# Block-sorted attention and a feed-forward on one core: sorting keys and values of batches 1 to 3 as rows, in tiles of the array, with crossbar transposes behind

## Chip, cores, metric

The kernel runs on 1 core of one Trainium2 chip. The metric is the device time of one execution in microseconds. Beside it stands the span of a profiled execution, from its first to its last instruction.

## What is computed

An attention over blocks with a learned soft sort, followed by a feed-forward over all tokens (3072 of them, 512 to 2048 features and back). There are 4 batches, 8 heads, 768 tokens and 64 features a head. Each head's tokens fall into 8 blocks of 96; an 8 x 8 matrix P (five rounds of normalising `sort_net` by rows and columns) mixes the blocks of keys and values, and then block i of the queries attends to mixed block i alone.

```python
def _attn_ref(q, k, v, sort_net):
    ...
    k_sorted = np.einsum('bhij,bhjcd->bhicd', P, k_b).reshape(B, H, S, D)
    v_sorted = np.einsum('bhij,bhjcd->bhicd', P, v_b).reshape(B, H, S, D)
    ...
    scores = scale * np.matmul(q_b, k_sb.transpose(0, 1, 2, 4, 3))
    scores = scores - np.max(scores, axis=-1, keepdims=True)
    attn = np.exp(scores)
    attn = attn / (np.sum(attn, axis=-1, keepdims=True) + 1e-09)
    return np.matmul(attn, v_sb).reshape(B, H, S, D).astype(np.float32)

def _moe_ref(x, w_in, w_out, s, b):
    h = x @ w_in
    r = np.maximum(h, 0.0)
    g = s * (r * r) + b
    return (g @ w_out).astype(np.float32)
```

## The kernel before

The feed-forward takes the tokens in eight tiles of 384, two a batch (`t = 2 * b` and `2 * b + 1`). `ffn1(t)` (line 395) makes 16 chunks of 128 hidden features, two per step, eight steps: 8 matmuls of 384 columns into a PSUM tile `hps`, a Relu on ScalarE (ACT) into `rt`, a squaring on VectorE (DVE) into `gt`. `ffn2(t)` (line 427) makes the output in three row groups of 128 tokens, each 16 matmuls of 512 columns into `ops`, followed by `store` (line 452): DVE scales `ops` into an `ot` tile (three buffers) and SP issues its DMA to `out`. Both take a table of slots: pieces of other work that are put into TensorE's stream after a step (`ffn1`) or after four matmuls (`ffn2`, slot = 4 * m + f // 4, so 12 slots in a call).

The attention of batch n = b + 1 is such other work: it lies in the slots of `ffn2(2 * b)` and `ffn2(2 * b + 1)`, and its result feeds `ffn1(2 * n)`. Each engine runs its instructions in the order in which they are written, with a wait at an instruction that needs another engine or a transfer. Batch 0's attention comes ahead of all that.

Attention of one batch:

- `load` (line 84) brings keys and values, cast to bf16, with partition = (head, block j, half z of the block) and 48 x 64 values in each; `load_q` (line 94) brings the queries in eight DMAs. GpSimd (POOL) issues these. For batches 2 and 3 they are behind `gated_loads` (line 555), whose small copy waits for the first `gt` of an earlier tile. Order in `loads` (line 508): k, v, q, then `v_sort`: eight copies on POOL that bring the values from (c, d) into (d, c) order, tile `VP`.
- `take_p` and `build_pd` (lines 219, 231) make `PD[b]`, a 128 x 128 matrix of weights from P, so that one matmul over the 128 partitions mixes the blocks of all heads. `jsel` and `bm` are masks for it; `emat` spreads P over the partitions.
- `k_piece` (line 247), three a batch: for each of 16 positions c, two matmuls with the raw keys as weights (128 x 64) and `PD` as the 64 moving columns. The result, keys with features on partitions, is in `tp`; the eviction reorders it into `KS`, where the 128 columns of one group g = (head pair, block) are contiguous (48 real and 16 zero columns, twice).
- `v_piece` (line 298), four a batch: for each of 16 features d, two matmuls with `VP` as weights and `PD` as 64 moving columns, into `tv`; the eviction reorders into `VS`, where a group's 64 features and two columns of ones lie side by side.
- `q_dma` (line 291): SP issues two DMA transposes of 96 x 2048 values through the crossbar, queries into `QT`.
- `s_piece` (line 311): 8 matmuls with weights from `KS` (64 rows x 128 columns) and 96 moving columns of `QT`; the two heads of a pair use the two halves of the rows. Then one Exp on ACT into `at`, 112 partitions.
- `p_piece` (line 342): 8 matmuls with `at` as weights and 66 moving columns of `VS`, then a reciprocal and a multiplication on DVE into `x`.
- `t_dma` (line 386): SP issues one DMA transpose of `x` into `xt`, which `ffn1` reads.

`KS`, `VP` and `VS` have two buffers each (`b % 2`). Tiles `tp`, `tv`, `sc`, `pv` and `hps` share three PSUM buffers of two banks (`psa`), taken in turn; `ops` has two of one bank (`psb`).

Of the kernel before, what the change touches and what calls it, by code (L numbers as in the profile page):

```python
# [22 lines left out]
def kernel(  # L23
# [33 lines left out]
    raw = [t.rearrange("b h (j z c) d -> b (h j z) (c d)", j=NB, z=2) for t in (q, k, v)]  # L57

    const = ctx.enter_context(tc.tile_pool(name="const", bufs=1))
    rawp = ctx.enter_context(tc.tile_pool(name="rawp", bufs=2))  # L60
# [23 lines left out]
    def load(t, b, parts=1):  # L84
# [3 lines left out]
        for c in range(0, C2, n):  # L88
            nc.gpsimd.dma_start(out=ti[:, c:c + n, :].rearrange("p c d -> p (c d)"),
                                in_=raw["qkv".index(t)][b][:, c * D:(c + n) * D])  # L90

    QTOK = {}

    def load_q(b, ns=range(NB)):
# [4 lines left out]
        for n in ns:  # L99
# [4 lines left out]
    nc.vector.memset(zeros[:, 128:512], 0.0)  # L104
    VP = [const.tile([128, D, GAP], BF, name=f"vp{i}") for i in range(2)]
    KS = [const.tile([128, NG, 2, GAP], BF, name=f"ks{i}") for i in range(2)]
    VS = [const.tile([KR, 2 * NG, VW], BF, name=f"vs{i}") for i in range(2)]
    nc.vector.memset(VP[0][:, :, C2:GAP], 0.0)
    nc.vector.memset(KS[0][:, :, :, C2:GAP], 0.0)
    nc.vector.memset(sne[:, NB, :], 1e-9)  # L110
# [6 lines left out]
    nc.gpsimd.memset(emat, 0.0)  # L117
    nc.gpsimd.affine_select(out=emat, in_=emat, pattern=[[-H, B], [-1, H], [0, 2 * NB]], base=0,
                            channel_multiplier=1, compare_op=ALU.not_equal, fill=1.0)
# [28 lines left out]

    def fill_vs(i):
        nc.gpsimd.memset(VS[i][:, :, D:VW], 1.0)  # L150
        nc.gpsimd.memset(VS[i][32:GAP, :, D:VW], 0.0)
        nc.gpsimd.memset(VS[i][32:C2, :, D:VW], 1.0)

    fill_vs(0)
    Z = []

# [7 lines left out]

    def permute(eng, b, src, cs=slice(0, C2), ds=slice(0, D)):
        o = VP[b % 2][:, ds, cs]
        i = src[:, cs, ds].rearrange("p c d -> p d c")
        if eng is nc.scalar:
            eng.copy(out=o, in_=i)
        else:  # L170
            eng.tensor_copy(out=o, in_=i)  # L171

# [3 lines left out]
    jsel = const.tile([128, NB], FP)  # L176
    bm = const.tile([128, 2 * 2 * NHP], FP)
    idle = [
        lambda: nc.vector.tensor_reduce(
# [9 lines left out]
    for it in range(5):  # L189
        nc.scalar.activation(out=sn, in_=sn, func=AF.Exp)  # L190
        if it >= 1:
            permute(nc.scalar, 0, v0f, slice((it - 1) * CV, it * CV))
# [25 lines left out]

    def take_p(b0, n, pe):

        bs = slice(b0, b0 + n)
        tmp = rtp.tile([128, n * NB, NB], FP, tag=f"tmp{n}", name="tmp")
        nc.vector.tensor_tensor(out=tmp, in0=pe.rearrange("p b i j -> p (b i) j"),
                                in1=spread(jsel, [[0, n * NB], list(jsel.ap[1])]), op=ALU.mult)
        nc.vector.tensor_reduce(out=PT[:, bs].rearrange("p b i -> p (b i)"), in_=tmp, axis=AX.X,
# [5 lines left out]
    def build_pd(b):  # L231
        pd = const.tile([128, 2, 2, NG], BF, name=f"pd{b}")
        nc.vector.scalar_tensor_tensor(
            out=pd.rearrange("p e z (a i) -> p (e z a) i", i=NB),
            in0=spread(bm, [list(bm.ap[1]), [0, NB]]), scalar=RC[:, b:b + 1],
            in1=spread(PT[:, b], [[0, 4 * NHP], list(PT.ap[2])]), op0=ALU.mult, op1=ALU.mult)
        PD[b] = pd

# [7 lines left out]

    def k_piece(b, c0, eng):
        src, mov, dst = RAW["k", b], PD[b], KS[b % 2]
        ps = psa.tile([128, CK, 2, NG], FP, tag="a", name="tp")
        for c in range(CK):  # L250
            for e in range(2):
# [3 lines left out]
                                 start=True, stop=True)  # L255
        evac(eng, dst[:, :, :, c0:c0 + CK], ps.rearrange("p c z g -> p g z c"))

    def q_tile(b):
# [38 lines left out]

    def v_piece(b, d0, eng):
        ps = psa.tile([128, CK, 2 * NG], FP, tag="a", name="tv")
        for d in range(CK):  # L300
            for z in range(2):
                nc.tensor.matmul(out=ps[z * GAP:(z + 1) * GAP, d, :],  # L302
                                 lhsT=VP[b % 2][:, d0 + d, :], rhs=PD[b][:, :, z, :],
                                 start=True, stop=True)
        evac(eng, VS[b % 2][:, :, d0:d0 + CK], ps[0:KR].rearrange("p d g -> p g d"))

# [4 lines left out]
    def s_piece(b, half, hp):  # L311
        g0 = hp * NB + half * HB
        sc = psa.tile([128, 2, 512], FP, tag="a", name="sc")
        for n in range(HB):
            for e in range(2):
                pr = slice(e * 64, (e + 1) * 64)
                nc.tensor.matmul(out=sc[:, e, n * BLK:(n + 1) * BLK],  # L317
                                 lhsT=KS[b % 2][pr, g0 + n].rearrange("p z c -> p (z c)"),
                                 rhs=QT[b][pr, half * HB + n, hp, :],
                                 start=True, stop=True)  # L320
        at = atp.tile([KR, 2, TG], BF, tag="at", name="at")
        nc.scalar.activation(out=at, in_=sc[0:KR, :, 0:TG], func=AF.Exp, scale=scale)  # L322
        AT[b, half, hp] = at

    def s_banks(b, half, hp):

        g0 = hp * NB + half * HB
        sc = [psb.tile([128, TG], FP, tag="b", name="scb") for _ in range(2)]
        for n in range(HB):
            for e in range(2):  # L330
                pr = slice(e * 64, (e + 1) * 64)
                nc.tensor.matmul(out=sc[e][:, n * BLK:(n + 1) * BLK],  # L332
                                 lhsT=KS[b % 2][pr, g0 + n].rearrange("p z c -> p (z c)"),
                                 rhs=QT[b][pr, half * HB + n, hp, :],
                                 start=True, stop=True)
        at = atp.tile([KR, 2, TG], BF, tag="at", name="at")
        for e in range(2):
            nc.scalar.activation(out=at[:, e], in_=sc[e][0:KR], func=AF.Exp, scale=scale)
        AT[b, half, hp] = at

    def p_piece(b, half, hp, later=False):
        g0 = hp * NB + half * HB
        atf = AT.pop((b, half, hp)).rearrange("p e t -> p (e t)")
# [4 lines left out]
        for e in range(2):  # L348
            for n in range(HB):
                c0 = (e * HB + n) * BLK  # L350
                m = 128 if c0 + 128 <= 2 * TG else BLK
                nc.tensor.matmul(out=pv[0:m, e, n * VW:(n + 1) * VW],  # L352
                                 lhsT=atf[:, c0:c0 + m], rhs=VS[b % 2][:, e * NG + g0 + n, :],
                                 start=True, stop=True)
# [103 lines left out]


    take_p(0, 1, spread_p(0, 1))  # L460
    build_pd(0)

# [4 lines left out]
    warm(3)  # L467
    k_piece(0, 0, "A")
    k_piece(0, CK, "D")
    k_piece(0, 2 * CK, "A")  # L470
    v_piece(0, 0, "D")
    v_piece(0, CK, "A")
    q_piece(0, 0, "D")
    v_piece(0, 2 * CK, "A")
    v_piece(0, 3 * CK, "D")
    s_piece(0, 0, 0)
# [31 lines left out]
    def loads(b):  # L508
        load("k", b)
        load("v", b)  # L510
        load_q(b)
        v_sort(b)

# [31 lines left out]
    def QB(b, n0, eng): return lambda: q_blocks(b, n0, eng)  # L545
# [16 lines left out]
    for b in range(B):  # L562
# [4 lines left out]
        if n == B:  # L567
# [44 lines left out]
```

## Time and profile before

| what | value |
|---|---|
| time, median of 3 runs | 228.32 us (227.29 to 228.38) |
| profiled execution: time, span | 228.41 us, 226.6 us |
| granted TensorE clock | 1.00 in every stretch |
| one batch in the steady part (start of `ffn2(0)` of one batch to the next) | 52.29, 102.30, 152.31: 50.01 us |
| of it `ffn1`, two tiles | 20.80 us |
| SP: DMA transposes of queries | 54.40 (two), 97.99 and 101.0, 148.0 and 150.7 |
| POOL: copies of `v_sort` | 52.90 to 59.34, 96.42 to 102.71, 146.29 to 152.57 |

The profile gives for each group of instructions its line, engine, operation, output and inputs, how many there were, the busy time, the mean of one in ns, and how long the engine sat idle before them and what ended that. Matmuls are pipelined, so the duration of a single one holds its way through the array; what a stream of them costs is read from the chain that ended last, which lists stretches by start and length. POOL's and SP's lines that end in `q` are the issuing of DMAs.

### The profile page before, as it was taken

The numbers are of one execution on the slowest core, as the hardware profiler recorded it, in microseconds if no ns is written. First come the engines' busy times: TensorE is split into PE (matmuls) and PEld (weight loads), VectorE is DVE, ScalarE is ACT, GpSimd is POOL, SyncE is SP. The second block draws the span as 40 slices with busy tenths as digits, with TensorE's granted clock in tenths as the row PEclk, the third lists the DMA queues.
The fourth block names the chain that finished last, engine by engine and source line by source line (L and its number), as shares of the span: only waits on it lengthen the run. The fifth ranks groups of instructions, "written<-read, shape, count | busy, mean of one in ns | idle before, by whom it ended". The sixth has DMA issues, their size and how long they took to land.

```text
span 226.6 us, 5806 instructions
## 1 busy us (share of the span) xinstructions
PE 218.9 (97%) x2542; PEld 133.2 (59%) x2542; DVE 124.5 (55%) x223; ACT 99.5 (44%) x128; POOL 68.2 (30%) x112
## 2 busy tenths in 40 slices
PE   7996999999999999999999999999999999999993
PEld 8985656655555556665555556655566566654452
DVE  6766467553647634498656634498557543441121
ACT  4966476564325225637143236627152246550000
POOL 8467797338400009291000028490000000000000
PEclk9999999999999999999999999999999999999999
DMA  5999999999711558993112459991123240001212
GB/s 190 238 105 133 181 164 206 207 196 136 164 49 49 129 151 136 188 166 72 49 47 73 138 120 176 176 171 36 49 95 67 100 114 0 4 0 46 94 49 93
DMA packets 53930, 25.82 MB, mean 114 GB/s; under 512 B 44944, under 2 KB 49296, under 8 KB 53904
## 3 DMA queue, kind: packets, MB, share of 16 engines
q0 software_dynamic: 30864, 12.85, 47.1%
q1 hardware_dynamic: 23040, 12.59, 20.9%
q8 instruction: 20, 0.33, 0.6%
q14 instruction: 6, 0.05, 0.1%
HBM read 27.27 MB, written 6.29 MB: 148 GB/s over the span
## 4 chain that ended last, share of the span: by engine, by line
PE 86%; DVE 5%; DMA 3%; POOL 2%; ACT 1%; issue 1%; POOLq 0%
PE ops L433 36%; PE hps L408 36%; PE pv L352 3%; PE tv L302 3%; DMA qtok<-in_q_dram 3%; PE sc L317 2%; PE tp L252 2%; PE ops L446 2%; POOL wi L131 1%; DMA sne<-in_sort_net_dram 1%; ACT rt L422 1%; POOL qtok L100 1%; ACT sne L190 1%; PE scb L332 1%; DVE rstat L200 0%
## 5 line engine op out<-in xcount | busy, mean ns | idle before, releaser
L408 PE MATMUL hps<-xt,wi 128*128 128x384 bf16 x512 | 85.7, 326 | 0.3 <-DMA qtok<-in_q_dram 0.3
L433 PE MATMUL ops<-wo,gt 128*128 128x512 bf16 x368 | 85.7, 379 | 0.0
L422 ACT ACTIVATE rt<-hps 128x768 bf16<-128x768 f32 x64 | 51.1, 811 | 53.4 <-PE hps L408 45.6
L423 DVE TENSOR_TENSOR gt<-rt 128x768 bf16<-128x768 bf16 x64 | 46.9, 739 | 41.2 <-ACT rt L422 40.4
L408 PEld LDWEIGHTS <-wi 128*128 128x128 bf16 x512 | 49.3, 98 | 33.5 <-issue 0.6
L433 PEld LDWEIGHTS <-gt 128*128 128x128 bf16 x368 | 33.7, 98 | 36.9 <-issue 0.6
L454 DVE SCALAR_TENSOR_TENSOR ot<-ops,s_bc,bias 128x512 f32<-128x512 f32 (+1 forms) x25 | 18.2, 730 | 30.8 <-PE ops L433 28.2
L322 ACT ACTIVATE at<-sc 112x768 bf16<-112x768 f32 x28 | 21.3, 808 | 30.3 <-PE sc L317 30.3
L100 POOL DMA_DIRECT2D qtok<-in_q_dram x32 | 24.9, 793 | 18.4 <-DMA rawv<-in_v_dram 9.0
L360 DVE TENSOR_TENSOR x<-pv,rec 96x512 bf16<-96x512 f32 x32 | 22.0, 687 | 1.1
L243 DVE CAST vs<-tv 112x1024 bf16<-112x1024 f32 x11 | 13.2, 1222 | 10.8 <-PE tv L302 10.7
L171 POOL COPY vp<-rawv 128x384 bf16<-128x384 bf16 x24 | 19.0, 849 | 0.0
L558 POOL COPY gate<-gt 128x1 bf16<-128x1 bf16 x2 | 0.4, 193 | 56.6 <-DVE gt L423 56.6
L352 PEld LDWEIGHTS <-at 112*128 112x128 bf16 (+1 forms) x256 | 12.8, 101 | 7.2 <-ACT at L322 1.1
L352 PE MATMUL pv<-vs,at 112*128 112x66 bf16 (+1 forms) x256 | 13.9, 195 | 1.0 <-DVE vs L243 1.0
L161 PE MATMUL z<-zeros 128*128 128x140 bf16 (+1 forms) x132 | 11.7, 256 | 1.2 <-DVE zeros L104 1.2
L302 PEld LDWEIGHTS <-vp 128*64 128x64 bf16 x512 | 9.0, 113 | 3.9 <-issue 3.6
L161 PEld LDWEIGHTS <-zeros 128*128 128x128 bf16 x132 | 10.1, 111 | 1.4 <-DVE zeros L103 1.0
L302 PE MATMUL tv<-pd,vp 128*64 128x64 bf16 x512 | 10.0, 197 | 0.9 <-issue 0.8
L241 ACT CAST ks<-tp 128x1024 bf16<-128x1024 f32 x8 | 8.1, 1012 | 4.0 <-PE tp L252 3.9
L131 POOL DMA_DIRECT2D wi<-in_moe_w_in_dram x16 | 8.6, 552 | 2.6 <-DMA wi<-in_moe_w_in_dram 0.9
L241 ACT CAST vs<-tv 112x1024 bf16<-112x1024 f32 x5 | 5.1, 1019 | 9.3 <-PE tv L302 9.3
(76 smaller groups left out, 104.3 us busy)
## 6 DMA issues: line engine op xcount, KB each, us to landing
out_dram<-ot SPq DMA_DIRECT2D x23, 256.0 KB, 2.0
qtok<-in_q_dram POOLq DMA_DIRECT2D x32, 96.0 KB, 9.5
rawk<-in_k_dram POOLq DMA_DIRECT2D x3, 768.0 KB, 6.8
rawv<-in_v_dram POOLq DMA_DIRECT2D x3, 768.0 KB, 10.0
wi<-in_moe_w_in_dram POOLq DMA_DIRECT2D x16, 128.0 KB, 5.2
wo<-in_moe_w_out_dram POOLq DMA_DIRECT2D x4, 512.0 KB, 10.8
v0f<-in_v_dram SPq DMA_DIRECT2D x4, 384.0 KB, 4.3
rawk<-in_k_dram POOLq DMA_DIRECT2D x3, 256.0 KB, 7.9
```

The source lines that it names most:

```text
L100: nc.gpsimd.dma_start(out=QTOK[b][:, n], in_=qv[:, n])
L161: nc.tensor.matmul(out=Z[0][:, 0:w], lhsT=zeros[:, 0:128], rhs=zeros[:, 0:w], start=True, stop=True)
L171: eng.tensor_copy(out=o, in_=i)
L302: nc.tensor.matmul(out=ps[z * GAP:(z + 1) * GAP, d, :], lhsT=VP[b % 2][:, d0 + d, :], rhs=PD[b][:, :, z, :], start=True, stop=True)
L322: nc.scalar.activation(out=at, in_=sc[0:KR, :, 0:TG], func=AF.Exp, scale=scale)
L352: nc.tensor.matmul(out=pv[0:m, e, n * VW:(n + 1) * VW], lhsT=atf[:, c0:c0 + m], rhs=VS[b % 2][:, e * NG + g0 + n, :], start=True, stop=True)
L360: nc.vector.tensor_tensor(out=x[:, :, hp * 128:(hp + 1) * 128].rearrange("p n (e d) -> p e n d", e=2), in0=pvv[:, :, :, 0:D], in1=rec.unsq ...
L408: nc.tensor.matmul(out=H1[i][:, f, 0:TG], lhsT=wi[:, hp, fc:fc + 128], rhs=xt[:, :, hp, :], start=(hp == 0), stop=(hp == NHP - 1))
L422: nc.scalar.activation(out=rt, in_=h, func=AF.Relu)
L423: nc.vector.tensor_tensor(out=gt[:, 2 * i:2 * i + 2, :], in0=rt, in1=rt, op=ALU.mult)
L433: nc.tensor.matmul(out=ops, lhsT=gt[:, f, m * 128:(m + 1) * 128], rhs=wo[:, f, :], start=(f == 0), stop=(f == NF - 1))
L454: nc.vector.scalar_tensor_tensor(out=ot[:, ns], in0=ops, scalar=s_bc, in1=BIAS[0][:, ns], op0=ALU.mult, op1=ALU.add)
```

## The change

Batch 0 stays as it is. In batches 1 to 3 keys and values are loaded with z as the slowest part of the partition, two DMAs of 64 partitions each (`load_z`), in the order k, q, v. `PD[b]` then is two 64 x 64 block matrices, one for each z, and it is the weights; the raw keys and values are the moving data. `k_rows` runs 16 matmuls a piece in tiles of 64 rows x 32 columns of the array, with 256 moving columns each; `v_rows` runs 4 in tiles of 64 x 64, with 384. The results have groups on the partitions, not features, so each piece is evicted into a staging place (`KO` and `VO`, batch 0's `KS` and `VP`), and SP issues DMA transposes of it into `KT` and `VT`: two for a piece of keys (128 x 512 each), one for a piece of values (128 x 1024). `keys` and `values` give the score and value matmuls their operands out of these: 128 columns of `KT` that lie 32 elements apart, and 66 columns of `VT` that lie 64 elements apart. The second buffers and `v_sort` go; the Exp of batches 1 to 3 is on 96 partitions. The masks for the new order are made by `masks_z` in `ffn1(1)`. The slots change: keys from slot 2 to 0, values from 5 and 9 to 6 and 8, the first `p_piece` from slot 11 of the first `ffn2` to slot 2 of the second, and `p_piece`s in pairs.

```diff
+    rawz = [t.rearrange("b h (j z c) d -> b z (h j) (c d)", j=NB, z=2) for t in (q, k, v)]
...
+    def load_z(t, b):
+        ti = rawp.tile([128, C2, D], BF, tag=f"raw{t}", name=f"raw{t}")
+        RAW[t, b] = ti
+        for z in range(2):
+            nc.gpsimd.dma_start(out=ti[z * 64:(z + 1) * 64].rearrange("p c d -> p (c d)"),
+                                in_=rawz["qkv".index(t)][b, z])
...
-    VP = [const.tile([128, D, GAP], BF, name=f"vp{i}") for i in range(2)]
-    KS = [const.tile([128, NG, 2, GAP], BF, name=f"ks{i}") for i in range(2)]
-    VS = [const.tile([KR, 2 * NG, VW], BF, name=f"vs{i}") for i in range(2)]
-    nc.vector.memset(VP[0][:, :, C2:GAP], 0.0)
-    nc.vector.memset(KS[0][:, :, :, C2:GAP], 0.0)
+    VP = const.tile([128, D, GAP], BF)
+    KS = const.tile([128, NG, 2, GAP], BF)
+    VS = const.tile([KR, 2 * NG, VW], BF)
+    nc.vector.memset(VP[:, :, C2:GAP], 0.0)
+    nc.vector.memset(KS[:, :, :, C2:GAP], 0.0)
+    KT = const.tile([128, 32, 128], BF)
+    VT = const.tile([128, D // 2 + 1, 128], BF)
+    KO = KS.rearrange("p g z c -> p (g z c)")[:, 0:C2 * D]
+    VO = VP.rearrange("p d c -> p (d c)").rearrange("p (d k) -> p d k", k=128)
...
-    nc.gpsimd.affine_select(out=emat, in_=emat, pattern=[[-H, B], [-1, H], [0, 2 * NB]], base=0,
+    nc.gpsimd.affine_select(out=emat[:, 0], in_=emat[:, 0], pattern=[[-1, H], [0, 2 * NB]], base=0,
...
+    for z in range(2):
+        em = emat[:, 1:B, z * 64:(z + 1) * 64]
+        nc.gpsimd.affine_select(out=em, in_=em, pattern=[[-H, B - 1], [-1, H], [0, NB]], base=-H,
+                                channel_multiplier=1, compare_op=ALU.not_equal, fill=1.0)
...
+    def masks_z():
+        nc.vector.tensor_reduce(
+            out=jselz, in_=ident.rearrange("p (z h j) -> p j z h", z=2, h=H), axis=AX.XY, op=ALU.add)
+        nc.vector.tensor_reduce(
+            out=bmz.rearrange("p (e a) -> p e a", e=2),
+            in_=ident.rearrange("p (z a e j) -> p e a z j", z=2, a=NHP, e=2), axis=AX.XY, op=ALU.add)
...
     def build_pd(b):
-        pd = const.tile([128, 2, 2, NG], BF, name=f"pd{b}")
+
+        m = bmz if b else bm
+        pd = const.tile([128, m.shape[1], NB], BF, name=f"pd{b}")
         nc.vector.scalar_tensor_tensor(
-            out=pd.rearrange("p e z (a i) -> p (e z a) i", i=NB),
-            in0=spread(bm, [list(bm.ap[1]), [0, NB]]), scalar=RC[:, b:b + 1],
-            in1=spread(PT[:, b], [[0, 4 * NHP], list(PT.ap[2])]), op0=ALU.mult, op1=ALU.mult)
-        PD[b] = pd
+            out=pd, in0=spread(m, [list(m.ap[1]), [0, NB]]), scalar=RC[:, b:b + 1],
+            in1=spread(PT[:, b], [[0, m.shape[1]], list(PT.ap[2])]), op0=ALU.mult, op1=ALU.mult)
+        PD[b] = (pd.rearrange("p (e a) i -> p e (a i)", e=2) if b else
+                 pd.rearrange("p (e z a) i -> p e z (a i)", e=2, z=2))
...
+    def k_rows(b, i, eng):
+
+        src = RAW["k", b]
+        ps = psa.tile([128, 2, CK // 4, 2, D], FP, tag="a", name="ko")
+        for e in range(2):
+            for x in range(4):
+                for z in range(2):
+                    zs, xs = slice(z * 64, (z + 1) * 64), slice(x * 32, (x + 1) * 32)
+                    nc.tensor.matmul(out=ps[xs, z, :, e, :], lhsT=PD[b][zs, e, :],
+                                     rhs=src[zs, i * CK + x:(i + 1) * CK:4, :],
+                                     start=True, stop=True, tile_position=(z * 64, x * 32))
+        ko = KO.rearrange("p (z m) -> p z m", z=2)[:, :, i * 512:(i + 1) * 512]
+        evac(eng, ko, ps.rearrange("p z c e d -> p z (c e d)"))
+        kt = KT[:, 0:C2 // 2].rearrange("p (z n) g -> p z n g", z=2)
+        for z in range(2):
+            nc.sync.dma_start_transpose(out=kt[:, z, i * 4:(i + 1) * 4, :], in_=ko[:, z])
+
+    def v_rows(b, i, eng):
+
+        src, n = RAW["v", b], D // 8
+        ps = psa.tile([128, 2, 512], FP, tag="a", name="vo")
+        for y in range(2):
+            for z in range(2):
+                zs, ys = slice(z * 64, (z + 1) * 64), slice(y * 64, (y + 1) * 64)
+                nc.tensor.matmul(out=ps[ys, z, 0:C2 * n], lhsT=PD[b][zs].rearrange("p e g -> p (e g)"),
+                                 rhs=src[zs, :, 2 * n * i + y:2 * n * (i + 1):2],
+                                 start=True, stop=True, tile_position=(z * 64, y * 64))
+        vo = VO[:, n * i:n * (i + 1), :]
+        evac(eng, vo[:, :, 0:BLK].rearrange("p d (z c) -> p z d c", z=2),
+             ps[:, :, 0:C2 * n].rearrange("p z (c d) -> p z d c", d=n))
+        nc.sync.dma_start_transpose(out=VT[:, n * i:n * (i + 1), :],
+                                    in_=vo.rearrange("p d k -> p (d k)"))
+
+    def keys(b, hp, n):
+
+        g = hp * NB + n
+        if b == 0:
+            return KS[:, g].rearrange("p z c -> p (z c)")
+        return KT.rearrange("p k (x g) -> p g (k x)", g=NG)[:, g]
+
+    def values(b, e, hp, n):
+        g = e * NG + hp * NB + n
+        if b == 0:
+            return VS[:, g, :]
+        return VT[0:BLK].rearrange("p d (y g) -> p g (d y)", y=2)[:, g]
+
+    def rows(b):
+        return BLK if b else KR
...
     def s_piece(b, half, hp):
-        g0 = hp * NB + half * HB
         sc = psa.tile([128, 2, 512], FP, tag="a", name="sc")
         for n in range(HB):
             for e in range(2):
                 pr = slice(e * 64, (e + 1) * 64)
                 nc.tensor.matmul(out=sc[:, e, n * BLK:(n + 1) * BLK],
-                                 lhsT=KS[b % 2][pr, g0 + n].rearrange("p z c -> p (z c)"),
+                                 lhsT=keys(b, hp, half * HB + n)[pr],
                                  rhs=QT[b][pr, half * HB + n, hp, :],
                                  start=True, stop=True)
-        at = atp.tile([KR, 2, TG], BF, tag="at", name="at")
-        nc.scalar.activation(out=at, in_=sc[0:KR, :, 0:TG], func=AF.Exp, scale=scale)
+        at = atp.tile([KR, 2, TG], BF, tag="at", name="at")[0:rows(b)]
+        nc.scalar.activation(out=at, in_=sc[0:rows(b), :, 0:TG], func=AF.Exp, scale=scale)
         AT[b, half, hp] = at
...
                 nc.tensor.matmul(out=pv[0:m, e, n * VW:(n + 1) * VW],
-                                 lhsT=atf[:, c0:c0 + m], rhs=VS[b % 2][:, e * NG + g0 + n, :],
+                                 lhsT=atf[:, c0:c0 + m], rhs=values(b, e, hp, half * HB + n),
                                  start=True, stop=True)
...
-    nc.gpsimd.memset(VP[1][:, :, C2:GAP], 0.0)
-    nc.gpsimd.memset(KS[1][:, :, :, C2:GAP], 0.0)
-    fill_vs(1)
+    nc.gpsimd.memset(KT[:, C2 // 2:, :], 0.0)
+    nc.gpsimd.memset(VT[:, D // 2, :], 1.0)
...
-    def v_sort(b):
-        for i in range(8):
-            permute(nc.gpsimd, b, RAW["v", b], ds=slice(i * 8, (i + 1) * 8))
-
     def loads(b):
-        load("k", b)
-        load("v", b)
+        load_z("k", b)
         load_q(b)
-        v_sort(b)
+        load_z("v", b)
...
-    def K(b, i, eng): return lambda: k_piece(b, i * CK, eng)
-    def V(b, i, eng): return lambda: v_piece(b, i * CK, eng)
...
-    ffn1(1, {-2: [TP(0, 1, 2, "D")], 1: [lambda: take_p(1, B - 1, PB), PDB(1)], 4: [PDB(2)],
+    ffn1(1, {-2: [TP(0, 1, 2, "D")], 1: [masks_z, lambda: take_p(1, B - 1, PB, jselz), PDB(1)], 4: [PDB(2)],
...
         q_dma(n)
         s0 = {
-            2: [K(n, 0, "A"), K(n, 1, "D"), K(n, 2, "A")],
-            5: [V(n, 0, "D"), V(n, 1, "A"), V(n, 2, "D")],
-            9: [V(n, 3, "D"), SC(n, 0, 0), SC(n, 0, 1)],
-            11: [P(n, 0, 0), SC(n, 0, 2), SC(n, 0, 3)]}
+            0: [K(n, 0, "A"), K(n, 1, "D"), K(n, 2, "A")],
+            6: [V(n, 0, "D"), V(n, 1, "A")],
+            8: [V(n, 2, "D"), V(n, 3, "A")],
+            10: [SC(n, 0, 0), SC(n, 0, 1)],
+            11: [SC(n, 0, 2), SC(n, 0, 3)]}
         ffn2(2 * b, s0)
-        ffn2(2 * b + 1, {0: [P(n, 0, 1)], 1: [P(n, 0, 2)],
-                         2: [P(n, 0, 3), TD(n, 0), SC(n, 1, 0), SC(n, 1, 1)],
-                         4: [P(n, 1, 0)], 5: [P(n, 1, 1), SC(n, 1, 2), SC(n, 1, 3)],
-                         7: [P(n, 1, 2)], 8: [P(n, 1, 3), TD(n, 1)]})
+        ffn2(2 * b + 1, {2: [P(n, 0, 0), P(n, 0, 1)],
+                         4: [P(n, 0, 2), P(n, 0, 3), TD(n, 0)],
+                         5: [SC(n, 1, 0), SC(n, 1, 1)], 6: [SC(n, 1, 2), SC(n, 1, 3)],
+                         8: [P(n, 1, 0), P(n, 1, 1)],
+                         10: [P(n, 1, 2), P(n, 1, 3), TD(n, 1)]})
```

More of the change, by code (lines that the diff above doesn't have):

```diff
@@ L147, in load_w @@
             nc.gpsimd.dma_start(out=wo[:, fs, :], in_=wov[:, fs, :])
[L149 to L154, printed above, removed]
+    nc.gpsimd.memset(VS[:, :, D:VW], 1.0)
+    nc.gpsimd.memset(VS[32:GAP, :, D:VW], 0.0)
+    nc.gpsimd.memset(VS[32:C2, :, D:VW], 1.0)
+    for z in range(2):
+        em = emat[:, 1:B, z * 64:(z + 1) * 64]
+        nc.gpsimd.affine_select(out=em, in_=em, pattern=[[-H, B - 1], [-1, H], [0, NB]], base=-H,
+                                channel_multiplier=1, compare_op=ALU.not_equal, fill=1.0)
     Z = []
@@ L162, in warm, with permute @@
                              start=True, stop=True)
[L165 to L171, printed above, removed]
+    def permute(cs):
+        nc.scalar.copy(out=VP[:, :, cs], in_=v0f[:, cs, :].rearrange("p c d -> p d c"))
     rstat = const.tile([BH, NB], FP)
@@ L177 @@
     bm = const.tile([128, 2 * 2 * NHP], FP)
+    jselz = const.tile([128, NB], FP)
+    bmz = const.tile([128, 2 * NHP], FP)
     idle = [
@@ L191 @@
         if it >= 1:
-            permute(nc.scalar, 0, v0f, slice((it - 1) * CV, it * CV))
+            permute(slice((it - 1) * CV, it * CV))
         if it in (1, 2):
@@ L217, in spread_p, with take_p @@
         return pe
-    def take_p(b0, n, pe):
+    def masks_z():
[4 more added lines that the diff above has]
+            in_=ident.rearrange("p (z a e j) -> p e a z j", z=2, a=NHP, e=2), axis=AX.XY, op=ALU.add)
+    def take_p(b0, n, pe, sel):
         bs = slice(b0, b0 + n)
@@ L223, in take_p @@
         nc.vector.tensor_tensor(out=tmp, in0=pe.rearrange("p b i j -> p (b i) j"),
-                                in1=spread(jsel, [[0, n * NB], list(jsel.ap[1])]), op=ALU.mult)
+                                in1=spread(sel, [[0, n * NB], list(sel.ap[1])]), op=ALU.mult)
         nc.vector.tensor_reduce(out=PT[:, bs].rearrange("p b i -> p (b i)"), in_=tmp, axis=AX.X,
@@ L245, with k_piece @@
     QT = {}
-    def k_piece(b, c0, eng):
-        src, mov, dst = RAW["k", b], PD[b], KS[b % 2]
+    def k_piece(c0, eng):
+        src, mov, dst = RAW["k", 0], PD[0], KS
         ps = psa.tile([128, CK, 2, NG], FP, tag="a", name="tp")
@@ L296, in q_dma, with v_piece @@
                 in_=QTOK[b][:, n0:n0 + HB].rearrange("p n h d -> p (n h d)"))
-    def v_piece(b, d0, eng):
+    def v_piece(d0, eng):
         ps = psa.tile([128, CK, 2 * NG], FP, tag="a", name="tv")
@@ L302, in v_piece @@
                 nc.tensor.matmul(out=ps[z * GAP:(z + 1) * GAP, d, :],
-                                 lhsT=VP[b % 2][:, d0 + d, :], rhs=PD[b][:, :, z, :],
+                                 lhsT=VP[:, d0 + d, :], rhs=PD[0][:, :, z, :],
                                  start=True, stop=True)
-        evac(eng, VS[b % 2][:, :, d0:d0 + CK], ps[0:KR].rearrange("p d g -> p g d"))
+        evac(eng, VS[:, :, d0:d0 + CK], ps[0:KR].rearrange("p d g -> p g d"))
     AT = {}
@@ L317, in s_piece @@
                 nc.tensor.matmul(out=sc[:, e, n * BLK:(n + 1) * BLK],
-                                 lhsT=KS[b % 2][pr, g0 + n].rearrange("p z c -> p (z c)"),
+                                 lhsT=keys(b, hp, half * HB + n)[pr],
                                  rhs=QT[b][pr, half * HB + n, hp, :],
                                  start=True, stop=True)
-        at = atp.tile([KR, 2, TG], BF, tag="at", name="at")
-        nc.scalar.activation(out=at, in_=sc[0:KR, :, 0:TG], func=AF.Exp, scale=scale)
+        at = atp.tile([KR, 2, TG], BF, tag="at", name="at")[0:rows(b)]
+        nc.scalar.activation(out=at, in_=sc[0:rows(b), :, 0:TG], func=AF.Exp, scale=scale)
         AT[b, half, hp] = at
     def s_banks(b, half, hp):
-        g0 = hp * NB + half * HB
         sc = [psb.tile([128, TG], FP, tag="b", name="scb") for _ in range(2)]
@@ L332, in s_banks @@
                 nc.tensor.matmul(out=sc[e][:, n * BLK:(n + 1) * BLK],
-                                 lhsT=KS[b % 2][pr, g0 + n].rearrange("p z c -> p (z c)"),
+                                 lhsT=keys(b, hp, half * HB + n)[pr],
                                  rhs=QT[b][pr, half * HB + n, hp, :],
                                  start=True, stop=True)
-        at = atp.tile([KR, 2, TG], BF, tag="at", name="at")
+        at = atp.tile([KR, 2, TG], BF, tag="at", name="at")[0:rows(b)]
         for e in range(2):
-            nc.scalar.activation(out=at[:, e], in_=sc[e][0:KR], func=AF.Exp, scale=scale)
+            nc.scalar.activation(out=at[:, e], in_=sc[e][0:rows(b)], func=AF.Exp, scale=scale)
         AT[b, half, hp] = at
     def p_piece(b, half, hp, later=False):
-        g0 = hp * NB + half * HB
         atf = AT.pop((b, half, hp)).rearrange("p e t -> p (e t)")
@@ L457, in store @@
         nc.sync.dma_start(out=out[r0:r0 + 128, ns], in_=ot[:, ns])
-    take_p(0, 1, spread_p(0, 1))
+    take_p(0, 1, spread_p(0, 1), jsel)
     build_pd(0)
@@ L467 @@
     warm(3)
[L468 to L472, printed above, removed]
+    k_piece(0, "A")
+    k_piece(CK, "D")
+    k_piece(2 * CK, "A")
+    v_piece(0, "D")
+    v_piece(CK, "A")
     q_piece(0, 0, "D")
-    v_piece(0, 2 * CK, "A")
-    v_piece(0, 3 * CK, "D")
+    v_piece(2 * CK, "A")
+    v_piece(3 * CK, "D")
     s_piece(0, 0, 0)
@@ L535, in make_bias, with K, V @@
         nc.scalar.activation(out=bias, in_=bps, func=AF.Copy, scale=b_bc)
-    def K(b, i, eng): return lambda: k_piece(b, i * CK, eng)
-    def V(b, i, eng): return lambda: v_piece(b, i * CK, eng)
+    def K(b, i, eng): return lambda: k_rows(b, i, eng)
+    def V(b, i, eng): return lambda: v_rows(b, i, eng)
     def SC(b, h, i): return lambda: s_piece(b, h, i)
```

## Prediction

> **What bounds the kernel now.** I read the busy times first, then the chain that ended last, then that chain by time through one steady batch, then single rows for the prices. Columns of the chain: start, length, engine, tile, line, count.
>
> ```profile
> PE 218.9 (97%) x2542; PEld 133.2 (59%) x2542; DVE 124.5 (55%) x223; ACT 99.5 (44%) x128; POOL 68.2 (30%) x112
> ...
> PE 86%; DVE 5%; DMA 3%; POOL 2%; ACT 1%; issue 1%; POOLq 0%
> ```
>
> TensorE is busy 97% of the span and makes 86% of the chain, so work taken from or given to TensorE in the steady part moves the end one for one, and work on other engines only where TensorE comes to wait for it. One batch of the steady part, 102.30 to 152.31 (three groups of the chain, from three places):
>
> ```profile
> 47.75 0.98 PE cps L527 x16
> ...
> 102.30 2.59 PE ops L433 x12
> 104.89 1.64 PE tp L252 x96
> 106.53 2.70 PE ops L433 x12
> 109.23 1.64 PE tv L302 x96
> 110.86 3.56 PE ops L433 x16
> 114.42 0.63 PE tv L302 x32
> 115.05 0.45 PE sc L317 x16
> ...
> 119.01 0.27 PE pv L352 x8
> ...
> 131.51 20.80 PE hps L408 x128
> ```
>
> There is no gap between the pieces: each starts where the last one ended. The sort of keys and values is 1.64 + 1.64 + 0.63 = 3.91 us of TensorE in each of batches 1 to 3. A lone matmul's price comes from two groups: ops takes 2.59/12 = 215.8 ns at 512 columns, hps 20.80/128 = 162.5 ns at 384, so 0.417 ns a column and 2.5 ns beside it. Against this, cps (four column tiles of the array, 512 columns) takes 0.98/16 = 61 ns a matmul, 3.5 at once. sc (two row tiles, 96 columns, 42.5 ns alone) takes 28 ns, two at once with 8 x 42.5 = 0.34 us and 0.11 us for going in and out of the tiled form. tp (two column tiles, 64 columns, 29.2 ns alone) takes 17 ns, also two at once.
>
> **The new sort on TensorE.** Keys: 3 pieces of 16 matmuls over 256 columns (109 ns alone), in 2 row x 4 column tiles. Eight at once gives 2 rounds a piece: 6 x 0.109 = 0.65, plus 0.11 for the form = 0.76. Two at once, the pairs of sc and tp, would be 24 x 0.109 + 0.11 = 2.73. Values: 4 pieces of 4 matmuls over 384 columns (162.5 ns), in 2 x 2 tiles: four at once 4 x 0.1625 + 2 x 0.11 = 0.87; two at once 1.52; one at a time 2.82. Row tiles overlap in sc and column tiles in cps, so I take full overlap: 0.76 + 0.87 = 1.63, which saves 3.91 - 1.63 = **2.28 us a batch**. Pairs alone would lose 0.34 a batch (2.73 + 1.52 - 3.91).
>
> **What reads the sorted data.** This is the hidden part. Today the evictions write the sorted rows so that each TensorE operand is contiguous. Now keys() takes 128 weight columns 64 bytes apart in KT, and values() takes 66 moving columns 128 bytes apart in VT. No TensorE row of this trace has such a stride. The nearest rows are other engines':
>
> ```profile
> L322 ACT ACTIVATE at<-sc 112x768 bf16<-112x768 f32 x28 | 21.3, 808 | 30.3 <-PE sc L317 30.3
> ...
> L169 ACT CAST vp<-v0f 128x768 bf16<-128x768 f32 x4 | 6.0, 1510 | 0.0
> ...
> L241 ACT CAST ks<-tp 128x1024 bf16<-128x1024 f32 x8 | 8.1, 1012 | 4.0 <-PE tp L252 3.9
> ```
>
> The cast of v0f reads elements 256 bytes apart. From 808 ns at 768 and 1012 at 1024, ScalarE pays 0.80 ns an element and 196 ns beside; the strided read pays (1510 - 196)/768 = 1.71 ns, 2.1 times as much. So three prices for a pv matmul, 64 of them a batch, 66 columns, 30.0 ns now: unchanged (+0); half rate, 0.833 ns a column, 57.5 ns (+27.5 x 64 = 1.76 us a batch); or ScalarE's time for an element on TensorE too, 1.71 ns, 115.4 ns (+5.46). I take half rate, the ratio of the nearest row, and keep both ends. The strided weights: two loads go under the 42.5 ns of a pair in sc. Unchanged they cost nothing; if each load came to 42.5 ns and the two went one after the other, a pair would take 85, +42.5 x 32 pairs = 1.36 us a batch. In pv a 128-column load hides under 31 ns, so there is room; I take nothing and keep 1.36. The moving rows of the new value sort have pairs 4 bytes apart; doubled they would be 0.65 more a batch, and I take nothing, as a line of neighbours is still used there.
>
> The Trainium skill's page SBUF — State Buffer (Door 1: The DMA port swizzle) speaks against the change: lines of 16 bytes, a stride free up to 8 bf16, a penalty for each access in a new line. It names no price for TensorE; by it, unchanged reads are out and the sum lies at the second or third price. On the weights, TensorE: Matmul & The Clock Gate (Weight-path perf modes) lets the fast load of 128 columns read packed or strided columns; by it their cost stays nothing.
>
> **The crossbar and its queue.** Each transpose of today moves 96 x 2048 values:
>
> ```profile
> L294 SPq DMA_TRANSPOSE qt<-qtok x6: 1424/1443/1686, 54.4 to 150.7; - x6
> ...
> DMA to landing us min/median/max: 3.7/3.8/4.2
> ```
>
> SP is held 1.44 us and the data lands 2.36 us later. New in a batch: six of 128 x 512 (a third of the data) and four of 128 x 1024 (two thirds). By size they hold SP 0.48 and 0.96 us each; by count 1.44. I take size, since both old shapes are equal and cannot separate the two. Count from T, the start of ffn2(2b), with 0.863 us per slot of four ops. Key evictions (1.01 ACT, 1.22 DVE) end at T+2.1, 2.6, 3.1; the six issues end at T+5.0 and land at T+7.4. Scores start after 11 slots and both sorts, 9.49 + 1.63 = T+11.1: 3.7 spare. Values are sorted at T+6.8 and T+9.0; their issues, with one output store (0.33) between, end at T+12.2 and land at T+14.5; the first pv comes after 15 slots, 1.63 and 0.90 of sc, T+15.5: 1.0 spare. By count, keys land at T+13.1 (2.0 late), values at T+19.6 (4.1 late in all): 4.1 us a batch. Behind a late transpose on SP wait the output stores, whose three ot buffers give slack of two row groups.
>
> **Loads, POOL, DVE, ACT.** POOL loses eight copies of 0.85 us a batch and gains two load issues of 0.56. Those copies lock the DVE today:
>
> ```profile
> 96.68 6.44 DVE L423 TENSOR_TENSOR gt<-rt 128x768 bf16<-128x768 bf16 x1 [0.74 <-ACT rt L422]
> ```
>
> One squaring that elsewhere takes 0.56 us takes 6.44 while POOL copies (96.42 to 102.71), and the last Relu of that stage runs at 105 instead of 103. TensorE never waits for it, so its end saves nothing by itself, but it lets the key sort move from slot 2 to slot 0: the PSUM buffers that it needs come free with Relus that now end by about T+1. If that cover failed, TensorE would wait some 2 us a batch. Queries now load ahead of the values; the last load lands where the last query load lands today (101.0 in batch 2, T-1.3; 54.4 in batch 1, T+2.1), while the value sort needs it at T+6.8, so 4.7 us cover it. Key loads stay first. In batch 1, the query transposes (54.4) stand ahead of the key transposes on SP: two issues, to T+5.0, so keys land by T+10.2, still 0.9 ahead. masks_z is two reductions near 0.27 us on a DVE busy 6.2 of 10 us there: nothing, 0.54 without that cover. Value evictions shrink from 1024 to 768 columns, off the chain. The split emat runs on POOL, which waits 4.78 us before line 463: nothing. Fewer, paired pv groups: 0.03 us each, left out.
>
> **Sum.** -2.28 + 1.76 = -0.52 a batch, three batches: -1.6 us. Profiled span 226.6 -> 225.0; that run took 228.41, 1.8 around the span, and the median of three is 228.32, so against the median **226.8 us**. By its unknowns: 226.8 + 3 x 1.36 = 230.9 with slow weight loads; 226.8 + 3 x 0.65 = 228.8 with slow moving pairs.
>
> **Rivals.** (1) Strides cost TensorE nothing: 228.3 - 6.8 = **221.5**. For it: pv and sc have the load hidden today and the operand rates of TensorE are its own; against: the strided ScalarE row. (2) Slower: a strided moving column costs what it costs ScalarE, 1.71 ns. -2.28 + 5.46 = +3.18 a batch, **237.9**. It decides from the point where a column of pv costs more than 0.96 ns (2.28 us over 64 x 66 columns is 0.54, plus today's 0.417). For it: the same row read as a time, not a ratio; against: TensorE already takes columns at half ScalarE's price. (3) Transposes cost SP their count, not their size: 226.8 + 12.3 = **239.1**, seen as TensorE waiting for KT and VT. Against: their data is a third. (4) Tiles overlap only in pairs: 228.3 + 3 x (0.34 + 1.76) = 234.6; cps speaks against it.
>
> **Chances.** Forecast 0.37, rival 1 0.28, rival 2 0.22, rival 3 0.09, rival 4 0.04. 0.5% (1.1 us) is what a measurement here tells from no change (the three runs lie 0.5% apart). The forecast lies just past it: of its 0.37, 0.20 falls faster, 0.12 within, 0.05 slower. Faster 0.28 + 0.20 = 0.48, same 0.12, slower 0.40. The range reaches rival 1 with a little room and rival 2: 220.5 to 238.5; the forecast's own is 225.5 to 230.9.
>
> **What would show it.** Chain of the new profile: key sort near 0.25 us a piece; an 8-group of pv at 0.27 (rival 1), near 0.5 (forecast) or 0.9 (rival 2); a 16-group of sc still 0.45 or toward 0.8 (weights); KT or VT as releaser of TensorE, and transposes of 1.4 us on SP, for rival 3; no gt of 6 us. I am wrong if the stride price is neither, or if something new holds TensorE in a batch.

## The result, and the profile after

The changed kernel takes 257.45 us (median of 6 runs, 255.62 to 258.99) against 228.35 us before: ratio 1.128, interval 1.1216 to 1.1343. The prediction was 226.8 us with a range of 220.5 to 238.5; the time lies outside it, and a gain was forecast where a loss came. The profiled execution's span is 253.9 us, 27.3 more than before.

The chain that ended last, by engine, on the page of the changed kernel:

```profile
PE 78%; DMA 6%; SPq 5%; DVE 4%; ACT 3%; issue 3%
```

TensorE's share fell from 86% to 78%; transfers and SP's issuing hold 11%, where transfers alone had 3%. The chain in order of time through batch 3 of the changed kernel (start, length, engine, tile, line, count; "issue" is time in which an engine waited for nothing that the profile shows):

```profile
171.74 0.81 PE ops L503 x3
172.55 0.78 PE ko L290 x48
...
178.67 1.26 SPq L297
179.93 0.05 issue
180.02 1.22 SPq L297
181.24 0.05 issue
181.29 2.48 DMA KT<-KS
183.77 0.35 issue
184.12 0.47 PE sc L389 x8
...
186.66 3.37 DMA VT<-VP
190.03 1.23 issue
191.25 1.98 PE pv L422 x16
193.23 2.92 PE ops L503 x8
...
199.62 0.81 PE ops L503 x3
200.43 0.63 PE sc L389 x14
...
202.89 1.82 PE pv L422 x16
```

Four things are to be seen. The key sort takes 0.78 us, where tp took 1.64. A pv matmul takes 1.82/16 = 114 ns, where it took 0.27/8 = 34. A 16-group of sc takes 0.63, where it took 0.45. And the chain leaves TensorE twice, for KT and for VT; after the second wait eight ops take 2.92 us instead of 1.73. The stretches of the changed kernel around that wait show why (columns: busy time of PE, PEld, DVE, ACT, POOL, then granted clock, DMA share, GB/s):

```profile
182.00:192.00 10.00, 6.91 (x59) 3.74 (x60) 0.96 (x2) 3.22 (x5) 0.00 (x0) 1.00 0.85 197
192.00:196.00 4.00, 4.00 (x20) 2.12 (x19) 2.52 (x5) 0.00 (x0) 0.00 (x0) 0.57 0.00 0
```

TensorE was busy for 6.91 of 10 us, and then the granted clock is 0.57 for a while: the wait is paid a second time. The transposes, as the changed kernel's tile view has them:

```profile
L297 SPq DMA_TRANSPOSE KT<-KS x18: 1190/1258/2018, 59.0 to 181.3; - x18
...
L312 SPq DMA_TRANSPOSE VT<-VP x12: 1272/1286/2147, 67.5 to 188.0; - x12
...
L367 SPq DMA_TRANSPOSE qt<-qtok x6: 3061/3896/4768, 50.9 to 170.1; - x6
```

SP is held 1.26 us by a transpose of 128 x 512 and 1.29 by one of 128 x 1024 (medians): between these two, size hardly matters.

### The profile page after: what moved, and what is told of

It is laid out like the page before. It is cut to its first block, busy times and chain, and to the rows that moved or that the text cites. A ratio compares the mean times of both kernels' runs of the same rounds, so it can differ in the third digit from the quotient of the medians.

```text
span 253.9 us, 4881 instructions
## 1 busy us (share of the span) xinstructions
PE 232.9 (92%) x2040; PEld 141.4 (56%) x2062; DVE 109.1 (43%) x222; ACT 101.1 (40%) x131; POOL 51.3 (20%) x93
## 4 chain that ended last, share of the span: by engine, by line
PE 78%; DMA 6%; SPq 5%; DVE 4%; ACT 3%; issue 3%
PE hps L478 32%; PE ops L503 27%; PE pv L422 10%; SPq L297 3%; PE sc L389 3%; DMA VT<-VP 3%; DMA KT<-KS 2%; DMA v0f<-in_v_dram 1%; PE ops L516 1%; SPq L312 1%; PE tv L375 1%; PE ko L290 1%; ACT at L394 1%; PE vo L306 1%; ACT rt L492 1%
## 5 line engine op out<-in xcount | busy, mean ns | idle before, releaser
L493 DVE TENSOR_TENSOR gt<-rt 128x768 bf16<-128x768 bf16 x64 | 35.5, 557 | 47.9 <-ACT rt L492 47.7
L394 ACT ACTIVATE at<-sc 96x768 bf16<-96x768 f32 (+1 forms) x28 | 21.2, 803 | 46.7 <-PE sc L389 46.5
L422 PEld LDWEIGHTS <-at 96*128 96x128 bf16 (+3 forms) x256 | 24.6, 112 | 10.7 <-issue 7.6
L422 PE MATMUL pv<-VT,at 96*128 96x66 bf16 x192 | 23.8, 290 | 6.0 <-DMA VT<-VP 3.2
L429 DVE RECIPROCAL rec<-pv 96x8 f32<-96x8 f32 x32 | 6.5, 202 | 30.3 <-PE pv L422 30.3
L389 PE MATMUL sc<-qt,KT 64*128 64x96 bf16 x192 | 8.8, 236 | 6.2 <-DMA KT<-KS 6.2
L389 PEld LDWEIGHTS <-KT 64*128 64x128 bf16 x192 | 7.2, 156 | 11.8 <-issue 11.4
L265 ACT CAST VP<-vo 128x768 bf16<-128x768 f32 x6 | 4.8, 799 | 17.3 <-PE vo L306 17.3
L267 DVE CAST VP<-vo 128x768 bf16<-128x768 f32 x6 | 5.7, 958 | 7.8 <-PE vo L306 7.8
L265 ACT CAST KS<-ko 128x1024 bf16<-128x1024 f32 x6 | 5.8, 1015 | 1.4 <-PE ko L290 1.4
```

The costliest lines, as they stand in the source:

```text
L265: nc.scalar.copy(out=out, in_=in_)
L389: nc.tensor.matmul(out=sc[:, e, n * BLK:(n + 1) * BLK], lhsT=keys(b, hp, half * HB + n)[pr], rhs=QT[b][pr, half * HB + n, hp, :], start=Tr ...
L394: nc.scalar.activation(out=at, in_=sc[0:rows(b), :, 0:TG], func=AF.Exp, scale=scale)
L422: nc.tensor.matmul(out=pv[0:m, e, n * VW:(n + 1) * VW], lhsT=atf[:, c0:c0 + m], rhs=values(b, e, hp, half * HB + n), start=True, stop=True)
L493: nc.vector.tensor_tensor(out=gt[:, 2 * i:2 * i + 2, :], in0=rt, in1=rt, op=ALU.mult)
```

## The experiments

The length of a batch goes from one start of ops after hps to the next, in each profile's chain; the table has batch 2, which the loading of weights no longer disturbs. Each ratio is to the old kernel as measured beside that run (228.35 to 229.51 us).

| kernel | time, us | ratio to before (interval) | batch 2, us |
|---|---|---|---|
| before | 228.35 | | 50.0 |
| changed | 257.45 | 1.128 (1.1216 to 1.1343) | 58.6 |
| e1, neighbouring columns | 237.19 | 1.035 (1.0298 to 1.0407) | 52.0 |
| e5 (e2), nobody waits | 240.74 (243.84) | 1.055 (1.0503 to 1.059) | 53.8 |
| e6 (e3), both | 224.41 (226.42) | 0.985 (0.9799 to 0.99) | 47.9 |
| e4, merged transposes | 247.22 | 1.082 (1.0758 to 1.0882) | 54.3 |
| e9, loads k, v, q | 258.2 | 1.125 (1.1176 to 1.1319) | 58.7 |
| e8, value rows, copied | 225.56 | 0.989 (0.9842 to 0.9936) | 48.8 |
| e10, the same, on the DVE | 226.33 | 0.987 (0.9818 to 0.9928) | 48.8 |

**e1: columns side by side.**

```diff
-        return KT.rearrange("p k (x g) -> p g (k x)", g=NG)[:, g]
+        return KT.rearrange("p k m -> p (k m)")[:, g * 128:(g + 1) * 128]
...
-        return VT[0:BLK].rearrange("p d (y g) -> p g (d y)", y=2)[:, g]
+        return VT[0:BLK].rearrange("p d k -> p (d k)")[:, g * VW:(g + 1) * VW]
```

> keys() and values() take 128 and 66 neighbouring columns of KT and VT, not columns 32 and 64 apart, so batches 1 to 3 use wrong pairs of keys and values; every transpose and every wait on it stays. Theory 1, strides: a pv matmul falls from 114 ns to about 34 and a 16-group of sc from 0.63-0.86 us to 0.45, in all 3 x (5.1 + 0.7) = 17.5 us, so about 240 us. Theory 2, late transposes are the loss and the strides hide beside them: 252 us or more, and longer waits on KT and VT.

237.19 us, 20 us less: somewhat more than theory 1 said. In its chain by time pv and sc have their old prices:

```profile
132.35 0.45 PE sc L389 x16
...
136.04 0.54 PE pv L422 x16
```

A group also no longer reads all of VT, so the first pv may start a little earlier than in the changed kernel. The strides are a large real cost, and 8 us above the old kernel beside it (228.92) remain.

**e2 and e5: nobody waits for the transposes.** Both read a constant tile with the same strides; e5 fills it later.

```diff
+    W2 = const.tile([128, D // 2 + 1, 128], BF)
...
+    nc.gpsimd.memset(W2, 0.01)
...
-        return KT.rearrange("p k (x g) -> p g (k x)", g=NG)[:, g]
+        return W2[:, 0:32].rearrange("p k (x g) -> p g (k x)", g=NG)[:, g]
...
-        return VT[0:BLK].rearrange("p d (y g) -> p g (d y)", y=2)[:, g]
+        return W2[0:BLK].rearrange("p d (y g) -> p g (d y)", y=2)[:, g]
```

> keys() and values() read a constant tile with the same strides as before, so the attention of batches 1 to 3 leaves the sorted data out; the sort and all transposes still run, nobody waits for them. Theory 2, late transposes: the waits for KT and VT and the lower granted clock behind them go, about 16 us, so about 241 us, with pv still 114 ns. Theory 1, strides alone: 254 us or more. If both are real and add, e1 and e2 together take away the sum.

> As e2, with the constant tile filled on POOL behind the loads of batch 1, so that the start of the kernel is that of the changed kernel (in e2 and e3 the fill delayed the first spread of P by 1 us, the granted TensorE clock fell, and the feed-forward began 6.3 and 5.8 us later). The attention of batches 1 to 3 leaves the sorted data out. If that was all, 243.8 - 6.3 = 237.5 us.

243.84 and 240.74 us, the latter 3 above what was expected; its batch 1 takes 56.1 us where batches 2 and 3 take 53.8, which is most of the difference. There TensorE waits for the load of the values, as e5's chain shows, with a later pv group below it:

```profile
52.33 8.51 DMA rawv<-in_v_dram
60.84 0.04 issue
60.88 0.52 PE vo L307 x7
...
124.30 1.82 PE pv L423 x16
```

Without waits a batch is 4.8 us shorter, with pv still at 1.82 us a 16-group, and e5's mean granted clock is 1.00. Late transposes are a second real cost.

**e3 and e6: both.** e3 combines e1 and e2, e6 the same with the later fill.

> Constant tile and neighbouring columns at once: sort and transposes run, attention of batches 1 to 3 leaves the sorted data out. If stride and wait are all that went wrong and add up, what is left is the sort's saving of 2.2 us a batch on TensorE: 221 to 223 us. A third cause (loads, SP, evictions) would show as 226 us or more.

> As e3, with the same later fill: neighbouring columns, no wait, the sorted data left out. 226.4 - 5.8 = 220.6 us if strides and late transposes are the whole loss and the sort saves 2.2 us a batch; 226 us again if something else takes the 5 us.

226.42 and 224.41 us, both below the old kernel and both above what was expected, for reasons of their own: in e3 the first ops starts at 57.16 against 51.38, in e6 batch 1 takes 50.5 us, with a shorter wait for the same load. Batch 2 takes 47.9 us in both. That is 2.1 below the old kernel's 50.0: the sort's saving, nearly as predicted (2.28). The four batch lengths make a square: strides cost 5.9 us without waits (53.8 - 47.9) and 6.6 with them (58.6 - 52.0); waits cost 4.1 without strides and 4.8 with them. They nearly add, and step by step -2.1 + 5.9 + 4.8 = 8.6 is the whole change of batch 2.

e3's late start is shown in its timeline of TensorE and its stretches: the spread of P waited for a mask that POOL made behind the fill, and the granted clock was 0.66 behind it.

```profile
12.44 0.88 PE L232 MATMUL pe<-sne,emat 32*128 32x64 f32 x6 [1.02 <-POOL emat L173]
...
20.00:24.00 4.00, 1.66 (x42) 1.38 (x42) 1.23 (x1) 1.49 (x3) 2.36 (x5) 0.66 1.94 168
```

The same stretch of the changed kernel has a clock of 1.00.

**e4: fewer transposes.** Two a batch for the keys, behind the third eviction, and two for the values.

```diff
-        for z in range(2):
-            nc.sync.dma_start_transpose(out=kt[:, z, i * 4:(i + 1) * 4, :], in_=ko[:, z])
+        for z in range(2 if i == 2 else 0):
+            nc.sync.dma_start_transpose(out=kt[:, z], in_=KO.rearrange("p (z m) -> p z m", z=2)[:, z])
...
-        nc.sync.dma_start_transpose(out=VT[:, n * i:n * (i + 1), :],
-                                    in_=vo.rearrange("p d k -> p (d k)"))
+        if i % 2:
+            nc.sync.dma_start_transpose(out=VT[:, n * (i - 1):n * (i + 1), :],
+                                        in_=VO[:, n * (i - 1):n * (i + 1), :].rearrange("p d k -> p (d k)"))
```

> The same data in fewer transposes: two of 128 x 1536 for the keys, issued behind the third eviction, and two of 128 x 2048 for the values, 4 a batch in place of 10. If SP is held by the count (1.2 to 1.4 us each), the keys land some 4 us earlier and the waits shrink: about 247 us. If SP is held by the size, the six issues become two of three times the length that start a little later: 257 to 260 us.

247.22 us, as the count theory has it, but only the keys follow it. Three times their data holds SP 1.4 to 1.8 us instead of 1.26; twice the values' data holds it 1.8 to 3.4 us, with a median of 2.57, twice the 1.29 of before (tile view of e4):

```profile
L297 SPq DMA_TRANSPOSE KT<-KS x6: 1415/1618/1837, 60.9 to 170.0; - x6
...
L313 SPq DMA_TRANSPOSE VT<-VP x6: 1794/2565/3402, 65.2 to 176.9; - x6
```

A batch is 54.3 us, 0.5 above e5's, so in the steady part nearly all of the wait is gone. What SP gained lies in the keys: two issues hold it 3.3 us in batches 2 and 3 where six held it 7.7 and 8.6, so the last values of batch 2 land at T+16.6 (T: the batch's start) instead of T+19.5. Two issues for the values hold it about as long as four did. Why 128 x 2048 takes twice as long as 128 x 1024, when 128 x 512 and 128 x 1024 are alike, stays open.

**e7: the price of a step.** The constant tile again, another step in each half batch.

```diff
+    VSTEP = {(1, 0): 2, (1, 1): 4, (2, 0): 8, (2, 1): 16, (3, 0): 32, (3, 1): 12}
+    KSTEP = {(1, 0): 2, (1, 1): 4, (2, 0): 8, (2, 1): 16, (3, 0): 1, (3, 1): 12}
...
+        s = VSTEP[b, n // HB]
+        return W2[0:BLK].rearrange("p k m -> p (k m)")[:, 0:VW * s:s]
```

> As e5, the sorted data left out, but the operands' columns lie 2, 4, 8, 16, 32 and 12 elements apart for the moving values (batch 1 halves, batch 2 halves, batch 3 halves) and 2, 4, 8, 16, 1 and 12 for the weights of sc. Read per pv matmul of 66 columns, 34 ns side by side and 114 ns at a step of 64. If each line of 16 bytes costs its time: 34 at 2, about 60 at 4, about 114 at 8, 12, 16 and 32. If a step is free up to 16 bytes: 34 up to 8, 114 from 12. If TensorE pays by the byte distance: rising on to 32. For sc a 16-group: 0.45 us up to the step where a load outlasts the moving columns, about 0.63 beyond.

From e7's chain by time, 16-groups of pv with steps of 2, 4, 8, 16, 32 and 12 elements, and one of sc with a step of 4 and one with 8:

```profile
68.47 0.54 PE pv L428 x16
74.00 0.47 PE sc L395 x16
76.30 0.99 PE pv L428 x16
114.83 0.65 PE sc L395 x16
118.17 1.91 PE pv L428 x16
132.32 1.95 PE pv L428 x16
172.05 1.82 PE pv L428 x16
185.97 1.91 PE pv L428 x16
```

A matmul costs 34 ns at 2, 62 at 4 and 114 to 122 at 8 and beyond. Less 2.5 ns, a step of 4 (two columns in each 16 bytes, 33 lines) pays 1.80 ns a line, a step of 8 (66 lines) 1.77, and 32 the same within a few per cent. At 2 the 16.5 lines (29 ns) are as long as the columns themselves (27.5). From a step of 8 on, where every column has a line to itself, the price no longer rises. So the line of 16 bytes is the unit, and each costs about 1.75 ns, the 1.71 that ScalarE's strided row had shown. The page SBUF — State Buffer of the Trainium skill (Door 1: The DMA port swizzle) names the 16-byte line, as measured here, but lets a stride be free up to 8 bf16; on TensorE it is free up to 2 and costs its full price at 8. The weights of sc are hidden up to 4 and cost 0.6 to 0.65 a group from 8 on. This was one run.

**e8 and e10: a version from the findings.** Keys are sorted as before the change. Values are sorted as rows ahead of them (slots 0 and 2), with two transposes a batch, and loads come in the order v, k, q; copies then bring VT into VS, side by side, on otherwise free engines.

```diff
+    def v_side(eng, i, g0, g1):
+        n = D // 8
+        o = VS[:, g0:g1, 2 * n * i:2 * n * (i + 1)].rearrange("p g (d y) -> p g d y", y=2)
+        s = VT[0:KR, n * i:n * (i + 1), :].rearrange("p d (y g) -> p g d y", y=2)[:, g0:g1]
...
+            0: [V(n, 0, "D"), V(n, 1, "A")],
+            2: [V(n, 2, "D"), V(n, 3, "A"), lambda: q_dma(n)],
+            4: [K(n, 0, "A"), K(n, 1, "D"), K(n, 2, "A")],
+            6: [VC(n, "P", 0, 0, 32), VC(n, "P", 0, 32, 64), VC(n, "P", 1, 0, 32), VC(n, "P", 1, 32, 64)],
+            9: [VC(n, "A", 2, 0, 32), VC(n, "A", 2, 32, 64), VC(n, "D", 3, 0, 64)],
```

> Only the values are sorted as rows (first, at slots 0 and 2), with two transposes a batch; POOL, ACT and DVE then copy VT so that a group's features lie side by side, and the values are read as before the change; keys are sorted as before the change. If strides and the count of transposes are the causes, TensorE keeps the values' saving, 2.26 - 0.9 = 1.35 us a batch, and nothing else: 228.4 - 4.1 = 224.3 us. If the copies come late or POOL's copies hold the DVE, 229 us or more, with VS as the releaser of TensorE.

> As e8, but all four copies of VT are on the DVE (1.18 us for 1024 elements in e8, where POOL and ACT take 1.08 for 512), the first two at slot 8, the others behind the scores of slot 11, so that no Exp waits behind a copy. If the copies' place costs the 0.1 to 0.35 us a batch by which e8 misses 48.7, 225 us; if the DVE's output stores come late behind the copies, 226 us or more.

225.56 us against 228.59 for the old kernel beside it, and 226.33 against 229.51: both are a little faster than the old kernel, by 1.1 and 1.3%, and much faster than the changed one. Both intervals lie below 1, and they overlap each other. Batch 2 is 48.8 us, 1.2 under the old kernel (1.35 expected). From e8's chain by time:

```profile
102.73 0.47 PE vo L295 x7
...
107.34 1.64 PE tp L282 x96
...
114.26 0.45 PE sc L384 x16
...
118.82 0.54 PE pv L417 x16
```

Sort, scores and values have their low prices together. Moving the copies to the DVE (e10) changed nothing that can be measured; in its batch 1 (53.1 us against 50.5 in e8) the scores wait for the queries' transposes, which land at 66.1 us.

**e9: order of loads.**

```diff
         load_z("k", b)
+        load_z("v", b)
         load_q(b)
-        load_z("v", b)
```

> The changed kernel with its loads in the order k, v, q as before the change. In the changed kernel the query transposes hold SP 3.1 to 4.8 us each, as value loads run beside them, and in batch 1 they end at T+7.8, 5 us behind the first key eviction. If that order is a part of the loss, the two transposes take 1.44 us each again, SP is free at about T+6 in batch 1, and the time falls by 2 us or so, to 255.5 us. If not (the queries then land later by as much), no change: 257.5 us.

258.2 us, no change. The query transposes take 1.45 us again (median), so value loads beside them were what stretched them; but the queries land later, and the first key transpose starts at 60.12 (T+6.4, T being the start of ffn2(0)) against 58.98 (T+7.6), with T itself 2.3 us later: e9's granted clock is 0.66 from 20 to 24 us, long before anything that the edit moves. Batch 1 takes 61.2 us against 61.8, batch 2 58.7 against 58.6. The stretch is real and costs little or nothing.

## Why the prediction was wrong, step by step

- **The new sort on TensorE**: right. 0.76 predicted for the keys, 0.78 measured; 0.87 for the values, 0.92 to 0.96 (two groups of 0.45 to 0.49). Row and column tiles overlap together, eight at once. Pairs of moving values 4 bytes apart cost nothing, as taken.
- **What reads the sorted data**: the step that failed first. The term was taken at half rate, 57.5 ns a pv matmul, "the ratio of the nearest row"; measured are 114 ns. Rival 2's reading of the same row, as a time, gave 115.4. e1, e5 against e6, and e7 show it: +5.1 us a batch where 1.76 was put. The strided weights, taken at nothing, cost 0.18 us a 16-group, 0.7 a batch, inside the kept end of 1.36. The rule cited from the page TensorE: Matmul & The Clock Gate (Weight-path perf modes), that the fast load may read strided columns, did not make them free.
- **The crossbar and its queue**: failed too. SP's hold was taken by size (0.48 and 0.96 us); 1.26 and 1.29 were measured. Rival 3 had this by count, 4.1 us a batch late; e5 against the changed kernel gives 4.8, and e4 shows that fewer issues for the keys take nearly all of it away. Part of the 4.8 is the lower granted clock after the wait (in batch 3, eight ops at 2.92 us instead of 1.73), which no term of the sum held.
- **Batch 1**: its query transposes were put at 1.44 us each and end at T+7.5 instead of T+5.0, since value loads ran beside them; that batch lost 11.8 us, the others 8.6 and 8.2. Moving the loads back (e9) did not give it back.
- **Loads, POOL, DVE, ACT**: right, but for the cover of the values in batch 1. No squaring of 6.4 us is left (the mean is 557 ns), and the key sort at slot 0 waits for no buffer. But the values of batch 1 were put at T+2.1, with 4.7 us of cover. In the changed kernel their loads are issued at 49.0 and 49.6 and take 7.0 and 8.7 us to land, so the last lands between T+6.3 and T+6.9, and their sort starts at about T+6.9. In e1, e4, e5 and e6 they land at T+8.1 to T+9.1 and TensorE waits.
- **The rivals as alternatives**: strides at ScalarE's time and holds by count were priced and given 0.22 and 0.09, but each alone. Both held, and they add: -2.28 + 5.46 + 4.1 = 7.3 us a batch by the prediction's own prices, some 250 us. The range ended at 238.5, below rival 3's own 239.1, and no case combined the two. That was a fault of reasoning: they sit in different places, one in TensorE's reads and one in SP's queue, and neither hides the other.

## What to carry to other kernels

A layout change is paid where the data is read: before a strided operand goes to TensorE, count the 16-byte lines that it touches, at about 1.75 ns each for moving columns, against 0.417 ns a column. Small transposes on a queue were paid by their number here (1.26, 1.29 and 1.62 us for 128 x 512, 1024 and 1536), but not without limit (2.57 for 128 x 2048), so a piece-by-piece scheme that suits evictions can starve the matmul behind it. And rivals that sit on different resources are to be added, not chosen between.

## What the runs showed of the hardware

- A price read on another engine was good as a time here, not as a ratio: ScalarE 1.71 ns a strided element, TensorE 1.69 to 1.80 a line.
- The DVE copies the same strided layout at 1.18 us for 1024 elements a partition, about 1.15 ns each, faster than ScalarE (1.09 us for 512) and POOL (1.08 us for 512). From the tile view of e8:

```profile
L311 POOL COPY VS<-VT x12: 1064/1076/1858, 61.4 to 160.7; 112x512 bf16<-112x512 bf16 x12
L271 ACT COPY VS<-VT x6: 1065/1094/1208, 63.2 to 163.0; 112x512 bf16<-112x512 bf16 x6
L273 DVE COPY VS<-VT x3: 1168/1180/1509, 63.2 to 161.9; 112x1024 bf16<-112x1024 bf16 x3
```

- A wait of 1 us at the start of e3 ended in a start of the feed-forward 5.8 us later, with a granted clock of 0.66 from 20 to 24 us. How much of the 5.8 us is the clock's was not separated: TensorE also sits idle for 2.1 us at 19.6, with no releaser in the profile.
- A query transpose that runs beside the value loads held SP for 3.1 to 4.8 us in the changed kernel, instead of 1.43 to 1.61 in e9.
